# Decoding two layers: all K of batch 6 kept across the layers, one K tile of batch 7 parked in PSUM

## The chip, the cores and the metric

The kernel runs on one core of a Trainium2 chip. The metric is device time in microseconds of one launch. Five engines work beside each other, each with its own queue of instructions: TensorE (PE), VectorE (DVE), ScalarE (ACT), GpSimd (POOL) and SyncE (SP), which here issues all the large DMAs.

## The reference

One decoding step of 8 sequences through an attention block and an MLP block, and then through both again with the same weights and the same caches:

```python
x = x + _A_ref(_layernorm(x, axis=-1), A_k_cache, A_v_cache, A_wq, A_wo)
x = x + _B_ref(_layernorm(x, axis=-1), B_w1, B_b1, B_w2, B_b2)
x = x + _A_ref(_layernorm(x, axis=-1), A_k_cache, A_v_cache, A_wq, A_wo)
x = x + _B_ref(_layernorm(x, axis=-1), B_w1, B_b1, B_w2, B_b2)
```

`_A_ref` is x·wq, attention of 32 query heads over 4 heads of K and V (4096 positions of 128 numbers, float32), then ·wo; `_B_ref` is gelu(x·w1 + b1)·w2 + b2. K and V of one sequence ("batch") are 8 MB each; 8 batches make 128 MB. wq and wo are 16 MB each, w1 and w2 14 MB each. All of it is read once in each layer, but for what stays on the chip from the first layer to the second.

## The kernel before

**The arena.** SBUF holds one area of 52 half tiles. A tile is 128 x 2048 float32, 1 MB: half of the positions of one K or V head of one batch, so a batch has 8 tiles of K and 8 of V; a half tile is 0.5 MB. 48 halves take K, V and weights; the last 4 (`own`) hold rows and probabilities of the softmax, and in between also weights (those whose limit is `ALL`).

**The stream.** `stream` is the list of everything to be loaded, in order. `pump` takes its first piece, finds free halves of the needed number, and issues the DMA on SP; if none are free it stops until `release` frees some. A DMA waits, on SP's queue, for the last reader of its halves, and all later DMAs wait behind it. `CUTS` tells into how many tiles each K or V of a batch is cut: (4, 4) is two DMAs of four tiles.

**The order.** `plan` writes the steps of the attention, one K tile a step; V tiles follow `LAG_V` = 10 steps behind their K. Batches in `AT_ONCE` do all K, the softmax, and then all V. The first layer goes through batches 0 to 7, the second through 7 to 0. So what batches 7 and 6 leave in the arena is used again first: 8 tiles of K 7, 8 of V 7 and 7 of K 6 (`EXTRA`); one of these seven is copied into four PSUM banks (`park_tile`) and back into the arena in the second layer (`unpark`). Besides, the last half tile of wq stays in its own place (`spare`). This leaves 4 halves and the 4 own ones, 4 MB, through which wo, w1, w2 and wq (stages o0, i0, p0, q1) pass in pieces of 1 MB.

**PSUM.** Of eight banks of 512 columns, four hold the parked tile, two are the accumulators of `project`, `expand` and `values` in turn (tag `o`), one holds scores (`s`) and one is for transposes and small sums (`pt`).

**Where the layers meet.** `layernorm` transposes x into bank pt (L168, L169), VectorE copies it out as xnT (L170), one more matmul sums (L174, bank s), and `expand` begins (L235). While q1's second unit runs, `early` scores four K 7 tiles (`first`) and frees them.

Of the kernel before, what the change touches and what calls it, by code (L numbers as in the profile page):

```python
# [33 lines left out]
LAG_V = 10  # L34
# [53 lines left out]
class Kept:  # L88


    def __init__(self, ap):
        self.ap, self.cols = ap, ap.shape[1]

    def free(self):
        pass


@with_exitstack
def decode_layers(ctx: ExitStack, tc: tile.TileContext, x, kc, vc, wq, wo, w1, b1, w2, b2, out):
# [59 lines left out]
    def small_ps(tag):  # L159
        return ps_1.tile([P, CH], F32, tag=tag, name="sps")  # L160
# [4 lines left out]
    def layernorm(xr, rsum):  # L165
        pt = small_ps("pt")
# [9 lines left out]
        nc.vector.tensor_scalar(xc[:, 0:Q4], xr, pm[:, 0:1], None, op0=ALU.add)  # L176
# [35 lines left out]
    def tiles(name):  # L212
        i = 0
        while (name, i) in held:
            yield held.pop((name, i))
            i += 1
        if (*name, "end") in held:
            yield held.pop((*name, "end"))

    def expand(name, unit, rs, finish, hooks={}, last=None):  # L220
        for u in range(2):
            acc = ps_o.tile([P, CH], F32, tag="o", name="acc")
# [4 lines left out]
            for i, slot in enumerate(tiles((name, u))):  # L227
# [13 lines left out]
                if last and u == 1 and at == end:  # L241
                    last(slot.ap)
# [13 lines left out]
    def turned(row, nt):  # L256
        pt = small_ps("pt")
# [28 lines left out]
    def project(name, n_k, lhs, out_row, resid, rsum, hooks={}):  # L286
        y = ps_o.tile([P, CH], F32, tag="o", name="y")
# [15 lines left out]
        nc.vector.scalar_tensor_tensor(out_row, y[:, 0:Q4], 1.0, resid, op0=ALU.mult, op1=ALU.add, accum_out=rsum)  # L303
# [6 lines left out]
    def v_at(b, r):  # L310
        return b, r // NH, r % NH

    def scores(at, kt, spare=False):
        b, j, half = at
        if j == 0:
            st["ps", half] = ps_o.tile([P, CH], F32, tag="o", name="s_ps") if spare else small_ps("s")
# [4 lines left out]
        for g in range(NG):  # L321
            nc.tensor.matmul(ps[32 * g:32 * g + 32, :], qz[:, c:c + 32], kt[:, g * CH:(g + 1) * CH],  # L322
# [11 lines left out]
    def probs(b):  # L334
        pm = small_ps("pt")
# [10 lines left out]
    def turn(b, half):  # L346
# [3 lines left out]
        pp = small_ps("pt")  # L350
# [14 lines left out]
    def values(at, v):  # L365
        b, j, half = at
        if half == 0:
            st["O"] = ps_o.tile([P, CH], F32, tag="o", name="o_ps")
# [13 lines left out]
    def heads(b, j):  # L382
        po = small_ps("pt")
# [14 lines left out]
    def early(key):  # L398
        ap, done = ap_of(key)
        scores(key[1:], ap, spare=key[3] == 1)  # L400
        done()

    def plan(layer, order):

        steps = []
        for i, b in enumerate(order):
            n = i * NR
            whole = b in AT_ONCE[layer]
            steps.append((n + NR - whole, 1, ("probs", b)))
# [7 lines left out]
    def attention(order, keep, done=(), hooks={}):  # L417
        ready = []
        steps = [key for key in plan(st["layer"], order) if key not in done]
        for n, key in enumerate(steps):  # L420
# [27 lines left out]
    def park_tile():  # L448
        spot = ps_k.tile([P, W], F32, name="spot")
# [10 lines left out]
    def unpark(ap):  # L460
        spot = st.pop("spot")
# [131 lines left out]
```

## Time and profile before

| | us |
|---|---|
| median of 3 runs | 875.83 (875.03 to 875.86) |
| the profiled execution, its own time | 875.91 |
| its span from first to last instruction | 874.1 |
| TensorE busy | 540.9 (62%) |
| VectorE busy | 180.7 (21%) |
| ScalarE busy | 48.3 (6%) |
| loads' share of 16 DMA engines' span | 99.2% |

The profile counts an engine as busy only while it works. The DMA row is the mean over 16 DMA engines. The chain of waits goes back from the last instruction, at each step to what released it.

### The profile page before, as it was taken

What the parts mean: (1) busy time and instruction counts of PE and PEld (TensorE: products, weight loads), DVE (VectorE), ACT (ScalarE), POOL (GpSimd) and SP (SyncE); (2) the same over time, 40 slices, a digit from 0 to 9 for tenths busy, and PEclk for the clock granted to TensorE, in tenths of its full rate; (3) what the DMA queues carried; (4) which work ended last, traced back from release to release, by engine and by line L of the source; (5) the groups of instructions that cost most, each with busy time, mean ns of one, the idle gap of its engine ahead of it and who ended that gap; (6) DMA issues with size and microseconds to landing.
All of it is one profiled execution on the core that took longest, in us unless ns stands there. A gap on an engine that the chain in (4) does not pass through costs nothing.

```text
span 874.1 us, 8939 instructions
## 1 busy us (share of the span) xinstructions
PE 540.9 (62%) x3936; PEld 179.6 (21%) x3936; DVE 180.7 (21%) x586; ACT 48.3 (6%) x76; POOL 1.8 (0%) x12
## 2 busy tenths in 40 slices
PE   0557575655766766666757679855676655665655
PEld 0212121211212212222222122211121211222222
DVE  0002222313122322200100124412232313120110
ACT  0100000000000100000000100000000000000000
POOL 0000000000000000000000000000000000000000
PEclk9867778777777876869887889975778777777889
DMA  9999999999999999999999999999999999999997
GB/s 389 439 433 433 432 433 433 432 439 445 432 433 405 422 429 425 413 414 420 422 421 396 423 426 433 427 451 435 436 430 430 432 430 433 429 433 430 431 420 294
DMA packets 19911, 370.61 MB, mean 424 GB/s; under 512 B 2336, under 2 KB 2720, under 8 KB 4128
## 3 DMA queue, kind: packets, MB, share of 16 engines
q1 hardware_dynamic: 19728, 369.91, 99.2%
q8 instruction: 31, 0.51, 0.2%
q10 hardware_dynamic: 144, 0.13, 0.0%
q14 instruction: 8, 0.07, 0.0%
HBM read 369.90 MB, written 0.13 MB: 423 GB/s over the span
## 4 chain that ended last, share of the span: by engine, by line
DMA 76%; PE 18%; DVE 4%; issue 1%; ACT 1%; SPq 0%; ACTq 0%; DVEq 0%
DMA arena<-in_A_v_cache_dram 25%; DMA arena<-in_A_k_cache_dram 24%; DMA arena<-in_B_w_dram 17%; PE sps L322 5%; PE o_ps L372 5%; DMA arena<-in_A_wo_dram 5%; PE acc L235 4%; DMA arena<-in_A_wq_dram 3%; DMA x_row<-in_A_x_dram 3%; PE y L292 2%; DVE scr L377 1%; PE sps L384 1%; PE sps L353 1%; DVE arena L327 1%; DVE scr L375 0%
## 5 line engine op out<-in xcount | busy, mean ns | idle before, releaser
L322 PE MATMUL sps<-arena,qz 128*32 128x512 f32 x992 | 144.2, 708 | 92.4 <-DMA arena<-in_A_k_cache_dram 82.3
L372 PE MATMUL o_ps<-arena 128*32 128x512 f32 x1024 | 158.7, 735 | 26.3 <-DMA arena<-in_A_v_cache_dram 26.3
L292 PE MATMUL y<-arena,oT 128*32 128x256 f32 x960 | 76.6, 463 | 53.2 <-DMA arena<-in_A_wo_dram 30.3
L235 PE MATMUL acc<-arena,xnT 128*32 128x512 f32 (+3 forms) x524 | 82.3, 692 | 43.9 <-DMA arena<-in_B_w_dram 25.3
L377 DVE SCALAR_TENSOR_TENSOR scr<-o_ps,sel_t,scr 128x128 f32<-128x128 f32 x192 | 67.3, 351 | 6.8
L322 PEld LDWEIGHTS sps<-arena,qz 128*32 128x32 f32 x992 | 30.9, 125 | 180.9 <-issue 84.2
L327 DVE TENSOR_SCALAR_CACHE_REDUCE arena<-sps 128x512 f32<-128x512 f32 x31 | 21.4, 691 | 149.3 <-PE sps L322 149.3
L292 PEld LDWEIGHTS y<-arena,oT 128*32 128x32 f32 x960 | 31.5, 127 | 97.2 <-DMA arena<-in_A_wo_dram 34.2
L353 PE MATMUL sps<-ident,arena 128*128 128x128 f32 x128 | 30.7, 385 | 33.1 <-DVE oT L385 16.8
L372 PEld LDWEIGHTS o_ps<-arena 128*32 128x32 f32 x1024 | 31.3, 127 | 96.1 <-issue 67.2
L343 ACT ACTIVATE arena<-arena,bias 128x1024 f32<-128x1024 f32 x16 | 18.4, 1148 | 481.3 <-DVE scr L340 481.3
L384 PE MATMUL sps<-sel_h,scr 128*128 128x8 f32 x128 | 26.2, 277 | 26.8 <-DVE scr L377 23.2
L375 DVE TENSOR_SCALAR scr<-o_ps,sel_t 128x128 f32<-128x128 f32 x64 | 22.4, 351 | 92.2 <-PE o_ps L372 92.2
L235 PEld LDWEIGHTS acc<-arena,xnT 128*32 128x32 f32 x524 | 20.4, 125 | 96.4 <-issue 40.8
L384 PEld LDWEIGHTS sps<-sel_h,scr 128*128 128x128 f32 x128 | 20.3, 200 | 86.4 <-DVE scr L377 66.2
L353 PEld LDWEIGHTS sps<-ident,arena 128*128 128x128 f32 x128 | 19.8, 192 | 42.1 <-ACT arena L343 23.9
L385 DVE TENSOR_TENSOR oT<-sps,scr 128x8 f32<-128x8 f32 x64 | 11.0, 172 | 77.7 <-PE sps L384 77.7
L303 DVE SCALAR_TENSOR_TENSOR x_row<-y,x_row 128x256 f32<-128x256 f32 x4 | 1.7, 425 | 103.0 <-PE y L292 103.0
L359 DVE COPY arena<-sps 128x512 f32<-128x512 f32 x16 | 11.1, 692 | 44.7 <-PE sps L353 44.7
L168 PE MATMUL sps<-ident,x_row 128*128 128x128 f32 x16 | 4.6, 379 | 25.2 <-DMA x_row<-in_A_x_dram 23.5
L336 PE MATMUL sps<-scr,ones 128*128 128x128 f32 x32 | 7.8, 326 | 15.6 <-DVE scr L332 15.6
L361 PE MATMUL sps<-scr,ones 128*128 128x32 f32 x32 | 9.5, 390 | 12.5 <-DVE arena L359 12.5
(72 smaller groups left out, 133.2 us busy)
## 6 DMA issues: line engine op xcount, KB each, us to landing
arena<-in_B_w_dram SPq DMA_DIRECT2D x27, 1024.0 KB, 8.4
arena<-in_A_v_cache_dram SPq DMA_DIRECT2D x10, 2048.0 KB, 28.7
arena<-in_A_wo_dram SPq DMA_DIRECT2D x15, 1024.0 KB, 8.7
arena<-in_A_k_cache_dram SPq DMA_DIRECT2D x7, 2048.0 KB, 30.5
arena<-in_A_wq_dram SPq DMA_DIRECT2D x14, 1024.0 KB, 8.5
arena<-in_B_w_dram SPq DMA_DIRECT2D x2, 7168.0 KB, 44.9
arena<-in_A_k_cache_dram SPq DMA_DIRECT2D x11, 1024.0 KB, 28.1
arena<-in_A_k_cache_dram SPq DMA_DIRECT2D x2, 4096.0 KB, 25.2
```

Of the source, the lines that this page charges most:

```text
L235: nc.tensor.matmul(acc[32 * j:32 * j + 32, d0 - starts[j]:d1 - starts[j]], xnT[:, kt * B:kt * B + 32], slot.ap[:, c + d0 - a:c + d1 - a], ...
L292: nc.tensor.matmul(y[32 * j:32 * j + 32, 0:Q4], lhs[:, kt * B:kt * B + 32], slot.ap[:, c + j * Q4:c + (j + 1) * Q4], start=(kt == 0), stop ...
L322: nc.tensor.matmul(ps[32 * g:32 * g + 32, :], qz[:, c:c + 32], kt[:, g * CH:(g + 1) * CH], start=(j == 0), stop=(j == HKV - 1))
L327: nc.vector.tensor_scalar(st["row", b].ap[:, half * CH:(half + 1) * CH], ps, SCALE, None, op0=ALU.mult, op1=ALU.max, accum_out=st["mx", b] ...
L343: nc.scalar.activation(row, row, AF.Exp, bias=bias, scale=1.0, accum_out=ls)
L353: nc.tensor.transpose(pp[:, t * P:(t + 1) * P], row[:, c:c + P], ident)
L359: nc.vector.tensor_copy(dst, src)
L372: nc.tensor.matmul(o[32 * g:32 * g + 32, :], s[:, g], v[:, g * CH:(g + 1) * CH], start=(half == 0), stop=(half == NH - 1))
L375: nc.vector.tensor_scalar(r, o[:, 0:P], sel_t[:, 0:1], None, op0=ALU.mult)
L377: nc.vector.scalar_tensor_tensor(r, o[:, t * P:(t + 1) * P], sel_t[:, t:t + 1], r, op0=ALU.mult, op1=ALU.add)
L384: nc.tensor.matmul(po[:, 0:REP], r_s[j % 2], sel_h, start=True, stop=True)
L385: nc.vector.tensor_tensor(oT_v[:, j * REP:(j + 1) * REP, b], po[:, 0:REP], rl_s[b % 2][:, j * REP:(j + 1) * REP], ALU.mult)
```

## The change

Three things are moved. All 8 tiles of K 6 stay (one as before in the four PSUM banks). wq's last half tile no longer stays; in its place the first tile of K 7 (`stowed`) is laid down in three parts: its upper half in `spare`, its lower half in the banks s and o1 (`stow`). In the second layer `unstow` brings the two quarters back into a half of the arena, ahead of the last five pieces of wq, and the scores read this tile in four quarters from two places. PSUM tiles are now fixed banks: while o1 is taken, all accumulators are o0, and `layernorm` puts its small sums into bank pt instead of s. And the order: in the first layer V 6 and V 7 follow 16 steps behind their K, so all of K 7 stands ahead of V 6; in the second layer batch 5 goes at once, with V 5 cut into four pieces.

```diff
-LAG_V = 10
-EXTRA = 7
-AT_ONCE = range(6), range(5)
+LAG = {(0, 6): 16, (0, 7): 16}
+AT_ONCE = range(6), range(6)
-    (1, "k", 6): (2, 2, 2, 1, 1), (1, "v", 6): (1, 1, 2, 2, 2), (1, "k", 5): (1, 1, 1, 1, 2, 2), (1, "v", 5): (4, 4), (1, "k", 4): (4, 4),
+    (1, "k", 6): (2, 2, 2, 1, 1), (1, "v", 6): (1, 1, 2, 2, 2), (1, "k", 5): (1, 1, 1, 1, 2, 2), (1, "v", 5): (2, 2, 2, 2), (1, "k", 4): (4, 4),
...
+    spot = psum.tile([P, W], F32, name="spot")
+    bank = {n: psum.tile([P, CH], F32, name=f"bank_{n}") for n in ("o0", "o1", "pt", "s")}
+    turns = {"of": ("o0", "o1"), "n": 0}
+    def next_o():
+        turns["n"] += 1
+        return bank[turns["of"][turns["n"] % len(turns["of"])]]
...
-        pm = small_ps("s")
-        nc.tensor.matmul(pm[:, 0:1], neg_m, rsum, start=True, stop=True)
+        pm = pt[:, Q4:Q4 + 1]
+        nc.tensor.matmul(pm, neg_m, rsum, start=True, stop=True)
...
+        if (st["layer"], key) == (1, stowed):
+            return quarters(held["stowed"].ap) + quarters(spare), lambda: release(held.pop("stowed"))
...
+            lag = LAG[layer, b] if (layer, b) in LAG else 10
...
+    def stow(part):
+        ap, done = ap_of(stowed)
+        if part == 0:
+            nc.scalar.activation(spare, ap[:, SCW:W], AF.Copy)
+        elif part == 1:
+            nc.scalar.activation(bank["s"], ap[:, 0:CH], AF.Copy)
+        else:
+            turns["of"] = ("o0",)
+            nc.scalar.activation(bank["o1"], ap[:, CH:SCW], AF.Copy)
+            done()
+    def unstow(ap):
+        nc.scalar.activation(ap[:, 0:CH], bank["s"], AF.Copy)
+        nc.vector.tensor_copy(ap[:, CH:SCW], bank["o1"])
...
+    stowed = ("k", *k_at(B - 1, 0))
-    kept |= {("k", *k_at(B - 2, r)) for r in range(EXTRA)}
+    kept |= {("k", *k_at(B - 2, r)) for r in range(NR)}
...
-    weights("q1", wq, [[1] * 2 + [2] * 7, [2] * 7 + [1]], [ALL] * 2, (0, SCW))
+    weights("q1", wq, [[1] * 2 + [2] * 7, [2] * 4 + [1] + [2] * 3 + [1]], [ALL] * 2)
+    stream.insert(len(stream) - 5, ("stowed", 1, unstow, ALL, False))
...
-            expand("q0", W, rs, query_unit, last=lambda ap: nc.scalar.activation(spare, ap[:, ap.shape[1] - SCW:], AF.Copy))
-            held["q1", 1, "end"] = Kept(spare)
+            expand("q0", W, rs, query_unit)
+            last = attention(orders[0], kept, hooks={
+                ("k", *k_at(B - 2, NR - 1)): park_tile, stowed: lambda: stow(0),
+                ("turn", B - 1): lambda: (opened(), stow(1)), ("v", *v_at(B - 2, NR - 1)): lambda: stow(2)})
```

The last layer's second `project` also leaves out the row sums that nobody reads.

How the rows move. SP's queue at the end of the first layer's attention, before (128x2048 is one tile, 128x4096 two; the four single K tiles are K 6's last two and K 7's first two):

```order
L205 DMA arena<-in_A_k_cache_dram 128x2048 x4
L205 DMA arena<-in_A_k_cache_dram 128x4096
L205 DMA arena<-in_A_v_cache_dram 128x4096
L205 DMA arena<-in_A_k_cache_dram 128x2048
L205 DMA arena<-in_A_v_cache_dram 128x4096
L205 DMA arena<-in_A_k_cache_dram 128x2048
L205 DMA arena<-in_A_k_cache_dram 128x4096
L205 DMA arena<-in_A_v_cache_dram 128x4096 x5
L205 DMA arena<-in_A_v_cache_dram 128x2048 x2
```

The same place now:

```order
L197 DMA arena<-in_A_k_cache_dram 128x2048 x4
L197 DMA arena<-in_A_k_cache_dram 128x4096
L197 DMA arena<-in_A_k_cache_dram 128x2048 x2
L197 DMA arena<-in_A_k_cache_dram 128x4096
L197 DMA arena<-in_A_v_cache_dram 128x4096 x7
L197 DMA arena<-in_A_v_cache_dram 128x2048 x2
```

The pieces are the same; the last K pieces stand ahead of all V 6. SP's queue from q1 into the second layer's attention, before (128x1024 is a half tile):

```order
L205 DMA arena<-in_A_wq_dram 128x2048 x14
L205 DMA arena<-in_A_wq_dram 128x1024
L205 DMA arena<-in_A_k_cache_dram 128x2048 x4
L205 DMA arena<-in_A_v_cache_dram 128x2048
L205 DMA arena<-in_A_k_cache_dram 128x2048
```

And now:

```order
L197 DMA arena<-in_A_wq_dram 128x2048 x11
L197 DMA arena<-in_A_wq_dram 128x1024
L197 DMA arena<-in_A_wq_dram 128x2048 x3
L197 DMA arena<-in_A_wq_dram 128x1024
L197 DMA arena<-in_A_k_cache_dram 128x2048 x3
L197 DMA arena<-in_A_v_cache_dram 128x2048
L197 DMA arena<-in_A_k_cache_dram 128x2048
```

One half tile of wq comes in, one tile of K 6 goes. TensorE's queue in the layer normalization between p0 and q1, before, with what each row waits for (sps is a bank of tag pt, and for L174 and L183 the bank s):

```order
L168 MATMUL sps<-ident,x_row 128x128 [waits DVE_49]
L169 MATMUL sps<-neg_m,rsum 128x128
L168 MATMUL sps<-ident,x_row 128x128
L169 MATMUL sps<-neg_m,rsum 128x128
L174 MATMUL sps<-rsum,neg_m 128x1 [waits Activation_49]
L235 MATMUL acc<-arena,xnT 32x512 [waits DMAHW4_49,DVE_49]
```

And now:

```order
L160 MATMUL bank_pt<-ident,x_row 128x128 [waits DVE_49]
L161 MATMUL bank_pt<-neg_m,rsum 128x128
L160 MATMUL bank_pt<-ident,x_row 128x128
L161 MATMUL bank_pt<-neg_m,rsum 128x128
L166 MATMUL bank_pt<-rsum,neg_m 128x1 [waits DVE_49]
L225 MATMUL bank_o_67<-arena,xnT 32x512 [waits DMAHW4_49]
```

The wait for VectorE's copy of xnT has moved from the first matmul of `expand` to the small sum ahead of it.

## Rows read from the trace of the kernel before

**Rows 1.** The page: GB/s in 40 slices; the loads' queue: packets, MB, share.
```profile
GB/s 389 439 433 433 432 433 433 432 439 445 432 433 405 422 429 425 413 414 420 422 421 396 423 426 433 427 451 435 436 430 430 432 430 433 429 433 430 431 420 294
...
q1 hardware_dynamic: 19728, 369.91, 99.2%
```

**Rows 2.** The page: shares of the chain that ended last.
```profile
DMA 76%; PE 18%; DVE 4%; issue 1%; ACT 1%; SPq 0%; ACTq 0%; DVEq 0%
```

**Rows 3.** Stretches: length, busy by engine, granted clock, DMA share, GB/s.
```profile
40.00:270.00 230.00, 138.16 (x878) 42.84 (x878) 52.89 (x173) 12.32 (x18) 0.00 (x0) 0.76 1.00 432
395.00:400.00 5.00, 3.48 (x30) 1.65 (x30) 1.35 (x5) 0.66 (x3) 0.00 (x0) 1.00 1.03 420
410.00:460.00 50.00, 31.23 (x279) 10.82 (x278) 4.81 (x16) 1.88 (x3) 0.28 (x1) 0.83 1.01 421
465.00:470.00 5.00, 4.44 (x34) 2.67 (x26) 0.53 (x3) 0.00 (x0) 0.00 (x0) 0.50 1.03 420
470.00:475.00 5.00, 4.85 (x27) 1.14 (x26) 0.64 (x3) 2.05 (x4) 0.00 (x0) 0.84 1.00 395
475.00:480.00 5.00, 2.46 (x16) 0.36 (x16) 0.00 (x0) 0.00 (x0) 0.00 (x0) 0.85 0.98 354
```

**Rows 4.** Timeline of TensorE, end of o0: start, length, line, shapes, idle before.
```profile
391.34 1.93 PE L292 MATMUL y<-arena,oT 128*32 128x256 f32 x16 [0.55 <-DMA arena<-in_A_wo_dram]
393.83 1.07 PE L292 MATMUL y<-arena,oT 128*32 128x256 f32 x16 [0.56 <-DMA arena<-in_A_wo_dram]
395.12 0.64 PE L292 MATMUL y<-arena,oT 128*32 128x256 f32 x8 [0.22 <-DMA arena<-in_A_wo_dram]
396.40 0.64 PE L292 MATMUL y<-arena,oT 128*32 128x256 f32 x8 [0.64 <-DMA arena<-in_A_wo_dram]
```

**Rows 5.** Timeline of TensorE, V 6's last two tiles, then V 5's first four.
```profile
558.24 1.07 PE L372 MATMUL o_ps<-arena 128*32 128x512 f32 x8 [2.24 <-DMA arena<-in_A_v_cache_dram]
...
567.95 1.06 PE L372 MATMUL o_ps<-arena 128*32 128x512 f32 x8 [0.61 <-DMA arena<-in_A_v_cache_dram]
```

**Rows 6.** Timeline of TensorE in p1, the two pieces of 2 MB.
```profile
860.41 1.93 PE L292 MATMUL y<-arena,oT 128*32 128x256 f32 x32 [1.23 <-DMA arena<-in_B_w_dram]
865.32 1.94 PE L292 MATMUL y<-arena,oT 128*32 128x256 f32 x32 [2.98 <-DMA arena<-in_B_w_dram]
```

**Rows 7.** The chain from p0 into q1: start, length, what.
```profile
467.30 0.44 DVE x_row L303 x2
...
470.18 1.76 PE acc L235 x4
473.27 5.28 DMA arena<-in_A_wq_dram
...
493.68 11.48 DMA arena<-in_A_wq_dram
```

**Rows 8.** Timeline of TensorE in that layer normalization.
```profile
469.66 0.43 PE L174 MATMUL sps<-rsum,neg_m 128*128 128x1 f32 x2
```

**Rows 9.** Timeline, the layer normalization between o0 and i0.
```profile
397.11 0.42 DVE L303 SCALAR_TENSOR_TENSOR x_row<-y,x_row 128x256 f32<-128x256 f32 x1 [34.07 <-PE y L292]
...
399.07 1.05 PE L235 MATMUL acc<-arena,xnT 128*32 128x512 f32 x4 [0.20 <-DVE xnT L170]
```

**Rows 10.** Timeline of SP's queue from 467 to 474: first start, length, count.
```profile
467.29 6.31 SPq L205 DMA_DIRECT2D arena<-in_A_wq_dram  x2
```

**Rows 11.** Line 205: time from issue to landing over all its loads.
```profile
DMA to landing us min/median/max: 5.3/12.5/60.4
```

**Rows 12.** The page: DMA issues, count, KB each, median us to landing.
```profile
arena<-in_A_wo_dram SPq DMA_DIRECT2D x15, 1024.0 KB, 8.7
...
arena<-in_A_v_cache_dram SPq DMA_DIRECT2D x2, 4096.0 KB, 30.9
```

**Rows 13.** The page: VectorE's reads of an accumulator; count, busy, mean ns.
```profile
L377 DVE SCALAR_TENSOR_TENSOR scr<-o_ps,sel_t,scr 128x128 f32<-128x128 f32 x192 | 67.3, 351 | 6.8
```

**Rows 14.** Groups by line, VectorE's read of a whole accumulator bank.
```profile
L250 DVE TENSOR_SCALAR scr<-acc,rs 128x512 f32<-128x512 f32 (+1 forms) x8 | 5.5, 682 | 53.7 <-PE acc L235 53.5
```

More of the change, by code (lines that the diff above doesn't have):

```diff
@@ L85, in free @@
             self.arena.freed[self.i + e] = self.arena.clock
[L88 to L95, printed above, removed]
 @with_exitstack
@@ L165, in layernorm @@
     def layernorm(xr, rsum):
-        pt = small_ps("pt")
+        pt = bank["pt"]
         for i in range(2):
@@ L216, in tiles, with expand @@
             i += 1
-        if (*name, "end") in held:
-            yield held.pop((*name, "end"))
-    def expand(name, unit, rs, finish, hooks={}, last=None):
+    def expand(name, unit, rs, finish, hooks={}):
         for u in range(2):
-            acc = ps_o.tile([P, CH], F32, tag="o", name="acc")
+            acc = next_o()
             at = 0
@@ L256, in turned @@
     def turned(row, nt):
-        pt = small_ps("pt")
+        pt = bank["pt"]
         for i in range((nt + 3) // 4):
@@ L315, in scores @@
         if j == 0:
-            st["ps", half] = ps_o.tile([P, CH], F32, tag="o", name="s_ps") if spare else small_ps("s")
+            st["ps", half] = bank["o1" if spare else "s"]
         if j == 0 and half == 0:
@@ L334, in probs @@
     def probs(b):
-        pm = small_ps("pt")
+        pm = bank["pt"]
         nc.tensor.matmul(pm[:, 0:P], ones, dg_s, start=True, stop=True)
@@ L349, in turn @@
             st["S", b] = arena.take(own=True)
-        pp = small_ps("pt")
+        pp = bank["pt"]
         for t in range(T):
@@ L367, in values @@
         if half == 0:
-            st["O"] = ps_o.tile([P, CH], F32, tag="o", name="o_ps")
+            st["O"] = next_o()
         o = st["O"]
@@ L388, in decode_layers, with quarters @@
     pieces = {}
+    def quarters(ap):
+        return [ap[:, g * CH:(g + 1) * CH] for g in range(ap.shape[1] // CH)]
     def ap_of(key):
+        if (st["layer"], key) == (1, stowed):
+            return quarters(held["stowed"].ap) + quarters(spare), lambda: release(held.pop("stowed"))
         name, i = pieces[st["layer"], key] if (st["layer"], key) in pieces else pieces[0, key]
@@ L399, in early @@
         ap, done = ap_of(key)
-        scores(key[1:], ap, spare=key[3] == 1)
+        scores(key[1:], ap if key == stowed else quarters(ap), spare=key[3] == 1)
         done()
@@ L412, in plan @@
                 steps.append((n + r, 0, ("k", *k_at(b, r))))
-                steps.append((n + NR - 1, 3, ("v", *v_at(b, r))) if whole else (n + r + LAG_V, 3, ("v", *v_at(b, r))))
+                steps.append((n + NR - 1, 3, ("v", *v_at(b, r))) if whole else (n + r + lag, 3, ("v", *v_at(b, r))))
         steps.sort(key=lambda e: e[:2])
@@ L432, in attention @@
                 if key[0] == "k":
-                    scores(key[1:], ap)
+                    scores(key[1:], quarters(ap))
                 else:
@@ L533, in decode_layers @@
         expand(f"i{layer}", F // 2, rs, hidden_unit)
-        rsum = row_sums()
+        rsum = None if layer else row_sums()
         project(f"p{layer}", NFT, hT, x_row, x_row, rsum)
```

48 lines of the change are left out of this document (21 added, 27 removed).

## Prediction, before the changed kernel had run

> **What bounds the kernel now.** I read the page's rows on the loads first, then the chain, then the kernel in stretches, and last the timeline where the stretches show less than the usual rate. The loads' queue is busy for 99.2% of 16 engines' span, and brings in 369.91 MB [rows 1]. 76% of the chain that ended last is loads [rows 2]. So the time is the bytes, divided by the rate that their pieces get, plus the few places where the queue runs dry.
>
> The rate depends on how a piece is cut. While K and V come in pieces of 8 MB it is 432 GB/s; in i0 and p0, in pieces of 1 MB, 421 [rows 3]. Where TensorE waits for every piece, its starts give the price: a tile of 1 MB takes 393.83 - 391.34 = 2.49 us, half a tile 396.40 - 395.12 = 1.28 us [rows 4].
>
> One stretch is short of load: 395 and 354 GB/s from 470 to 480, where 421 are usual. That is (26 + 67) x 5 / 421 = 1.1 us of loading lost [rows 3]. Its cause is in the queue: SP issues one load at 467.29 and only one more within 6.31 us, at 473.27 [rows 7, 10]. In between lies the layer normalization between p0 and q1. No half of the arena comes free before q1's first matmuls are done: VectorE has x at 467.30, q1 begins at 470.18, and the load issued at 473.27 lands after 5.28 us, the least of all loads [rows 7, 11]. All other loads have more in front of them. So 5.28 us is what the queue must hold at an issue, about two tiles; the median is 8.7 in o0, and 11.48 at the end of q1 [rows 7, 12]. A delay of TensorE's by less than the difference costs nothing.
>
> **The change part by part.** *Bytes.* K 6's last tile is no longer loaded in the second layer: one tile of 1 MB, -2.49 us. wq's last half tile is loaded a second time: +1.28 us [rows 4]. V 5 comes in four pieces of 2 MB, not two of 4 MB. A piece of 4 MB took 567.95 - 558.24 = 9.71 us [rows 5], one of 2 MB 865.32 - 860.41 = 4.91 [rows 6], so +2 x (2 x 4.91 - 9.71) = +0.2 us. Sum: -1.0 us. These loads stand in an unbroken queue, so the whole of it reaches the end; the bounds are -1.4 (pieces of 2 MB as good as those of 4 MB, half a tile at half the price of a tile) and -0.6 (V 5 twice as dear).
>
> *The layer normalization.* The small sum L174 took 0.43 us on TensorE beside VectorE's copy of xnT (L170) [rows 8]. Both its output and the copy's input are now bank pt, so it waits for the copy, and q1's first matmul stands behind it. That adds 0.43 us and a handover to the chain from 467.30 to 470.18; I take 0.5. Queued behind it on TensorE are all matmuls of q1's first piece, and behind these SP's load of 473.27. There the queue is dry already, so all of it counts: +0.5 us. The same edit stands in the other three normalizations. At the start and in the second layer the loads are of 7 or 8 MB with tens of us in front of them; between o0 and i0 the slack is that of the 8.7 against 5.28 us. There it costs nothing. The bounds: 1.0, if the weights of this sum are loaded in series too; and below nothing, -1.1, all that the stretch loses now. For the chain's length goes with the clock that TensorE is granted: between o0 and i0, at 1.00 of 2.4 GHz, the same steps took 399.07 - 397.11 = 1.96 us, here, at 0.50, the level of 1.2 GHz, 470.18 - 467.30 = 2.88 [rows 3, 7, 9]. I take the nearest row, 0.43, at the clock that this place had.
>
> *One accumulator.* From the first layer's V 7 to the end of q1 every accumulator is bank o0, so a new one waits until VectorE has read the last. For an expansion's second unit that is one read of 0.68 us [rows 14], less what lay there anyway; for each head of V 7, and for o0's first matmul, four reads of 0.351 [rows 13], 1.4 us. A head of V 7 takes two tiles, 5 us of loading, and needs 1.4 us and two tiles of matmuls: TensorE keeps up. All these delays are under the 8.7 - 5.28 = 3.4 us that the queue has in hand: nothing. Without that cover each would cost its own length, 0.7 to 1.4 us at five places.
>
> *Stowing and bringing back.* Three copies on ScalarE in the first layer. ScalarE is idle nearly always there, and only the last of them frees a tile, one that o0's third piece takes. In q1, two copies of 512 columns, on ScalarE and VectorE, each about the 0.68 us of the read above, stand between q1's first piece of unit 1 and the first early scores; VectorE's copy also ahead of the queries' (L267). +0.7 us on TensorE at most. The tile frees half a tile now, not a whole one, and one K tile less stands behind wq: of 11.48 us in front of a load some 2.5 are gone and another 0.7 may be. That leaves 8.3, and 5.28 are needed: nothing.
>
> *K 7 ahead of V 6.* In the first layer the same pieces come in another order, and the slices there show 425 to 431 GB/s and none much below [rows 1]. There is little to gain and, with all of V 6 still to pass through the arena, more than ten us in the queue: nothing. V 5 ahead of K 4's pieces in the second layer: V 5's loads had 30.9 us in front of them [rows 12]: nothing.
>
> Sum: -1.0 + 0.5 = -0.5 us. The profiled execution took 875.91 us, 1.8 us more than its span, and is 0.08 above the median of 875.83. So 875.4 for it, and 875.3 for the median.
>
> Here a rule of the Trainium skill speaks against the change: in "DMA: Bandwidth & Descriptors", section "Anatomy of one DMA", a DMA (measured there for those that GpSimd issues) has a fixed cost of some 2.0 us beside its bytes. The change has two loads more (one tile of K fewer, half a tile of wq and two pieces of V 5 more). The trace of this kernel doesn't bear it out as a cost of each piece: tiles land 2.49 us apart [rows 4], and by the rule, an estimate, 1 MB alone would take 2.0 + 2.4 us. It is a latency here, hidden while another piece is in front.
>
> **The rivals.** *The dry stretch goes.* What decides it is how long TensorE takes from p0's last pieces to q1's first. If that part runs at the higher clock, as between o0 and i0, it is 0.9 us shorter [rows 3, 7, 9], and p0's last matmuls and q1's first with it; the load of 473.27 comes some 2 us earlier, and the 1.1 us aren't lost. For it: the two normalizations are alike in work, and their clocks differ. Against it: the new wait pushes the other way, and what TensorE does ahead of the place is unchanged. Time: -1.0 - 1.1 = -2.1, 873.8 us.
>
> *The queue runs dry in q1, too.* Place: q1's second unit. The tile that comes back takes half a tile of the little room, its scores wait for two copies, and the load behind it needs a whole pair of halves, so it waits for the next piece of wq. Price: nothing until loads there find under 5.28 us in front of them; from then on every us of delay is one of the time. From 8.3 us that needs 3 us of delay; with two such handovers of the room, each up to one piece late (2.49 us), 5 us are possible at most, and 2.5 are a middle. For it: with 4 halves and 4 more it is the narrowest place. Against it: 8.3 us by my count. Time: -0.5 + 2.5 = +2.0, 877.8 us.
>
> *It trades bytes and delays evenly.* The normalization costs 1.0 and V 5's cut 0.6: +-0, 875.8 us. For it: all terms are small, and the bounds meet there.
>
> *Each piece pays its latency.* A mechanism of the rows: a load alone takes 5.28 us, of which 2.49 are its bytes; if the 2.8 us aren't hidden, two more pieces cost 5.6, and the time is 880. Against it: nothing in the rows but the stretch after 470. By the skill's rule named above it would be two times 2.0.
>
> **How the numbers follow.** A measurement of this kernel can't tell less than 0.2%, 1.75 us, from no change. The forecast, 875.3, has 0.57; the dry stretch goes 0.19; even trade 0.15; dry in q1 0.07; latency of each piece 0.02. Of the second, whose 873.8 lies just past the bound of 874.1, some count as no change; in return, the forecast's own lower bound (-1.4 and a part of the 1.1) passes it now and then. Faster 0.18, within 0.2% 0.74, slower 0.08. The likeliest case reaches from 874.3 to 876.4 (-1.4 - 0 and -0.6 + 1.0, each with a little for the runs' own scatter). To leave out no more than 2 in 10, the range takes in the dry stretch's going and a little of the drying in q1: 873.2 to 877.0.
>
> **What would show it.** Right: the loads' queue brings 369.39 MB; K 5's first load lands some 0.7 us earlier than now (-2.49 + 1.28 + 0.5); from L166 to q1's first matmul some 0.4 us more than now; the stretch after 470 at 374 GB/s or less; all else near 421 and 432. Wrong: a second stretch under 400 GB/s, in q1's second unit or in the first layer's V 7; a load there that lands within 5.3 us of its issue; a drying that is gone; or a rate of whole stretches that changed.

## The result and the profile after

| | before | after |
|---|---|---|
| median of the runs side by side | 875.36 us (874.94 to 876.84, 21 runs) | 878.95 us (874.71 to 883.01, 21 runs) |
| ratio after to before, 95% interval | | 1.0039 (1.0026 to 1.0052) |
| profiled execution; its span | 875.91; 874.1 us | 880.35; 878.6 us |
| bytes of the loads' queue; its share | 369.91 MB; 99.2% | 369.38 MB; 98.6% |

The changed kernel is slower by 0.4%, and its runs spread over 8 us where those of before spread over 2. The forecast, 875.3 us and at most 877.0, was wrong. Of all executions in this document one, of 1150.91 us, of a kernel with q1's tiles in halves, was in a slow state and is left out.

The page of after, answering [rows 1]:

```profile
GB/s 387 437 430 430 430 455 436 433 427 427 433 425 421 421 430 426 357 421 419 421 420 416 383 423 428 437 445 428 433 433 427 430 445 425 433 427 433 431 421 264
...
q1 hardware_dynamic: 20016, 369.38, 98.6%
```

The bytes are as forecast. Two slices stand out, 357 and 383, at 1/40 of 878.6 us each: the end of the first layer's attention, and q1. The stretches of after there, with the columns of [rows 3]:

```profile
355.00:360.00 5.00, 3.37 (x17) 0.41 (x16) 1.57 (x5) 0.00 (x0) 0.00 (x0) 0.50 1.02 423
360.00:365.00 5.00, 3.36 (x26) 1.05 (x26) 1.57 (x5) 0.00 (x0) 0.00 (x0) 0.73 0.49 162
365.00:370.00 5.00, 3.79 (x62) 1.73 (x54) 0.17 (x1) 0.00 (x0) 0.00 (x0) 1.00 1.01 398
...
470.00:475.00 5.00, 3.92 (x26) 2.23 (x28) 0.91 (x4) 1.93 (x4) 0.00 (x0) 1.00 1.02 423
475.00:480.00 5.00, 2.72 (x22) 0.32 (x16) 0.16 (x1) 0.13 (x1) 0.00 (x0) 1.00 1.02 411
...
490.00:495.00 5.00, 4.02 (x20) 0.92 (x12) 1.44 (x3) 0.60 (x1) 0.00 (x0) 0.50 1.01 419
495.00:500.00 5.00, 4.54 (x28) 1.37 (x32) 0.47 (x2) 0.00 (x0) 0.00 (x0) 0.58 0.75 308
500.00:505.00 5.00, 5.00 (x48) 1.34 (x39) 1.23 (x1) 2.31 (x2) 0.00 (x0) 1.00 0.97 365
```

Measured against 421 GB/s, 360 to 370 us loses (259 + 23) x 5 / 421 = 3.3 us of loading, and 495 to 505 loses (113 + 56) x 5 / 421 = 2.0. The stretch after 470, which lost 1.1 us before [rows 3], loses only 0.1: here its clock was 1.00, before 0.84 and 0.85, behind a stretch of 0.50.

**The first place** is V 7, the last V of the first layer. TensorE's timeline there (L363 is the values' matmul, L375 a head's sum, L368 VectorE's reads of O, L280 the projection o0):

```profile
342.13 1.93 PE L363 MATMUL bank_o<-arena 128*32 128x512 f32 x8 [2.90 <-DMA arena<-in_A_v_cache_dram]
...
347.73 1.06 PE L363 MATMUL bank_o<-arena 128*32 128x512 f32 x8 [1.64 <-DVE scr L368]
...
352.61 1.94 PE L363 MATMUL bank_o<-arena 128*32 128x512 f32 x8 [1.63 <-DVE scr L368]
354.48 0.60 PE L375 MATMUL bank_pt<-sel_h,scr 128*128 128x8 f32 x2
355.00 1.94 PE L363 MATMUL bank_o<-arena 128*32 128x512 f32 x8
358.57 1.94 PE L363 MATMUL bank_o<-arena 128*32 128x512 f32 x8 [1.63 <-DVE scr L368]
...
364.49 1.93 PE L280 MATMUL bank_o<-arena,oT 128*32 128x256 f32 x32 [1.64 <-DVE scr L368]
```

At a clock of 0.50, the level of 1.2 GHz, a tile takes 1.94 us, and each head after the first waits 1.63 us for VectorE: 358.57 - 352.61 = 5.96 us for the third head, where two tiles load in 2 x 2.49 = 4.98 [rows 4]. From the first head to o0's first matmul it is 364.49 - 342.13 = 22.4 us, and the loads of four heads take 19.9. SP issued o0's first three tiles by 340.14. The fourth needs halves that V 7's last matmul sets free (360.96 + 1.89 = 362.85); it comes at 362.92, first of five within 6.3 us:

```profile
362.92 6.26 SPq L197 DMA_DIRECT2D arena<-in_A_wo_dram  x5
```

By then the queue had nearly run out: 162 GB/s.

**The second place** is q1's second unit. TensorE first, then two of SP's issues:

```profile
491.91 1.94 PE L225 MATMUL bank_o<-arena,xnT 128*32 128x512 f32 x8 [0.87 <-DVE scr L238]
...
495.46 1.06 PE L313 MATMUL bank_s<-arena,qz 128*32 128x512 f32 x2 [0.57 <-DVE qz L255]
...
497.14 1.96 PE L225 MATMUL bank_o<-arena,xnT 128*32 128x512 f32 x8
```

```profile
493.96 0.33 SPq L197 DMA_DIRECT2D arena<-in_A_wq_dram  x1
...
499.15 0.33 SPq L197 DMA_DIRECT2D arena<-in_A_wq_dram  x1
```

The unit waits 0.87 us for VectorE to read the first unit's sums out of the one bank, and everything up to 499 runs at half clock. The first early score is done when the next weights start, at 497.14; it frees half a tile, which no whole tile fits. SP's next issue is at 499.15, right behind the end of the next weights (497.14 + 1.96). 5.2 us without an issue are about as much as the queue held. The shortest time from issue to landing fell from 5.3 us [rows 11] to:

```profile
DMA to landing us min/median/max: 4.7/10.9/60.8
```

In the Trainium skill, "DMA: Bandwidth & Descriptors", section "Anatomy of one DMA", a DMA (measured there for those that GpSimd issues) costs some 2.0 us beside its bytes. 4.7 less the 2.49 of a tile leaves 2.2: the trace agrees for a load with next to nothing in front of it, and not for tiles in a filled queue, 2.49 us apart [rows 4].

**The end.** TensorE fell to half clock in p1's last tiles (a mean of 0.61 from 870 to 876), whose 64 matmuls then outlasted the loads:

```profile
868.64 6.61 PE L280 MATMUL bank_o<-arena,oT 128*32 128x256 f32 x64 [2.96 <-DMA arena<-in_B_w_dram]
...
875.78 0.35 SPq L551 DMA_DIRECT2D out_dram<-x_row  x1
```

The last 2 MB piece's matmuls start 868.64 - 865.32 = 3.3 us later than before [rows 6]. The kernel before lost a little at the two places, too: from 360 to 380 it moved 410 GB/s where the changed one moved 354, and 411 from 500 to 505:

```profile
360.00:380.00 20.00, 12.22 (x130) 4.53 (x130) 0.52 (x2) 0.00 (x0) 0.00 (x0) 0.73 1.01 410
```

So against it the first place costs (67 - 11) x 20 / 421 = 2.7 us and the second 2.0 - 0.1 = 1.9: -1.0 (bytes) - 1.0 (stretch after 470) + 2.7 + 1.9 = +2.6. The other 0.7 of the 3.3 isn't placed. The store is issued 875.78 - 871.42 = 4.4 us later, so the end itself added 1.0; before it was:

```profile
871.42 0.35 SPq L537 DMA_DIRECT2D out_dram<-x_row  x1
```

All together 3.3 + 1.0 = 4.3, against 880.35 - 875.91 = 4.4 measured. The 1.0 at the end goes with the execution and not with the change: behind the last load's landing the store came 2.3 us later here, 1.2 before, but 1.2 in the changed kernel's second profile and 2.3 in the kernel before with the new order (both below).

### The profile page after: what moved, and what is told of

Same layout as the page of the kernel before. It is cut to its first block, busy times and chain, and to the rows that moved or that the text cites. A ratio compares the mean times of both kernels' runs of the same rounds, so it can differ in the third digit from the quotient of the medians.

```text
span 878.6 us, 8957 instructions
## 1 busy us (share of the span) xinstructions
PE 548.7 (62%) x3936; PEld 182.2 (21%) x3936; DVE 181.8 (21%) x586; ACT 50.0 (6%) x79; POOL 1.8 (0%) x12
## 3 DMA queue, kind: packets, MB, share of 16 engines
q1 hardware_dynamic: 20016, 369.38, 98.6%
HBM read 369.38 MB, written 0.13 MB: 421 GB/s over the span
## 5 line engine op out<-in xcount | busy, mean ns | idle before, releaser
L313 PE MATMUL bank_s<-arena,qz 128*32 128x512 f32 x988 | 145.7, 721 | 92.4 <-DMA arena<-in_A_k_cache_dram 81.4
L363 PE MATMUL bank_o<-arena 128*32 128x512 f32 x1024 | 159.6, 741 | 20.8 <-DMA arena<-in_A_v_cache_dram 15.8
L280 PE MATMUL bank_o<-arena,oT 128*32 128x256 f32 x960 | 80.1, 485 | 50.5 <-DMA arena<-in_A_wo_dram 28.1
L225 PE MATMUL bank_o<-arena,xnT 128*32 128x512 f32 (+3 forms) x528 | 81.6, 687 | 41.7 <-DMA arena<-in_B_w_dram 21.9
L313 PEld LDWEIGHTS bank_s<-arena,qz 128*32 128x32 f32 x988 | 32.7, 127 | 188.6 <-issue 91.8
L368 DVE SCALAR_TENSOR_TENSOR scr<-bank_o,sel_t,scr 128x128 f32<-128x128 f32 x192 | 67.3, 350 | 6.8
L280 PEld LDWEIGHTS bank_o<-arena,oT 128*32 128x32 f32 x960 | 32.3, 133 | 97.6 <-DMA arena<-in_A_wo_dram 38.4
L344 PE MATMUL bank_pt<-ident,arena 128*128 128x128 f32 x128 | 30.3, 380 | 33.1 <-DVE oT L376 16.7
L363 PEld LDWEIGHTS bank_o<-arena 128*32 128x32 f32 x1024 | 30.8, 127 | 86.1 <-issue 58.8
L375 PE MATMUL bank_pt<-sel_h,scr 128*128 128x8 f32 x128 | 26.3, 278 | 28.7 <-DVE scr L368 24.8
L375 PEld LDWEIGHTS bank_pt<-sel_h,scr 128*128 128x128 f32 x128 | 20.5, 201 | 87.1 <-DVE scr L368 70.5
```

The source lines that it names most:

```text
L225: nc.tensor.matmul(acc[32 * j:32 * j + 32, d0 - starts[j]:d1 - starts[j]], xnT[:, kt * B:kt * B + 32], slot.ap[:, c + d0 - a:c + d1 - a], ...
L280: nc.tensor.matmul(y[32 * j:32 * j + 32, 0:Q4], lhs[:, kt * B:kt * B + 32], slot.ap[:, c + j * Q4:c + (j + 1) * Q4], start=(kt == 0), stop ...
L344: nc.tensor.transpose(pp[:, t * P:(t + 1) * P], row[:, c:c + P], ident)
L363: nc.tensor.matmul(o[32 * g:32 * g + 32, :], s[:, g], v[:, g * CH:(g + 1) * CH], start=(half == 0), stop=(half == NH - 1))
L368: nc.vector.scalar_tensor_tensor(r, o[:, t * P:(t + 1) * P], sel_t[:, t:t + 1], r, op0=ALU.mult, op1=ALU.add)
L375: nc.tensor.matmul(po[:, 0:REP], r_s[j % 2], sel_h, start=True, stop=True)
```

## The experiments

Medians with the ratio to the kernel before, run on the same chip (95% interval); before's medians there were 875.26 to 875.76.

| kernel | median us (range) | ratio |
|---|---|---|
| changed, two accumulators in V 7 | 876.53 (875.12 to 879.96) | 1.0018 (1.0008 to 1.0029) |
| changed, way back earlier on ScalarE | 877.69 (874.81 to 882.4) | 1.0029 (1.0014 to 1.0044) |
| changed, old order of loads | 887.39 (884.59 to 888.83) | 1.0125 (1.0111 to 1.0140) |
| before, new order of loads | 875.17 (875.01 to 876.06) | 0.9997 (0.9989 to 1.0006) |
| changed, both of the first two | 877.78 (876.19 to 880.13) | 1.0023 (1.0014 to 1.0032) |
| both, copy one head earlier | 876.6 (874.64 to 878.93) | 1.0011 (1.0001 to 1.0021) |
| the same kernel again | 877.47 (874.31 to 880.32) | 1.0021 (1.0008 to 1.0034) |
| the same, tiles of q1 in halves | 876.35 (874.06 to 879.80) | 1.0006 (0.9991 to 1.0020) |
| the same, two accumulators in q1 | 875.91 (874.64 to 878.15) | 1.0005 (0.9996 to 1.0014) |
| the same, both of these | 875.49 (874.12 to 879.53) | 0.9998 (0.9989 to 1.0006) |
| before, small sum in bank pt | 875.46 (875.07 to 876.46) | 1.0000 (0.9991 to 1.0009) |
| before, one accumulator in q1 | 875.34 (875.05 to 878.05) | 1.0002 (0.9994 to 1.0011) |

One kernel measured twice differs by 0.1%, so steps of that size between the changed variants tell nothing by themselves. A profile is of one execution; its clocks need not be those of the median.

### Two accumulators in V 7

```diff
-                ("turn", B - 1): lambda: (opened(), stow(1)), ("v", *v_at(B - 2, NR - 1)): lambda: stow(2)})
+                ("turn", B - 1): lambda: (opened(), stow(1)), ("v", *v_at(B - 1, NR - 1)): lambda: stow(2)})
```

> The changed kernel, with one edit: the tile's last quarter goes into bank o1 after the last V 7 tile, not after the last V 6 tile, so that V 7 has two accumulators again. Theory (one accumulator): in the profile of the changed kernel a head of V 7 took 5.96 us at the lower clock, more than the 4.9 us in which its two tiles land, so TensorE ended V 7 6 us after its last tile, no half came free, and loading fell to 162 GB/s from 360 to 365 (2.4 to 3.2 us). With two accumulators the dip at o0's start goes: 2 to 3 us faster than the changed kernel, about 876 to 877, the dip in q1 stays. Rival (order): TensorE is slow in V 7 because its work now comes in small portions at the lower clock; then V 7 stays late and the time stays at 879.

Measured 876.53. TensorE's timeline in V 7 shows the heads waiting for loads again, not for VectorE; only o0's first matmul still does:

```profile
346.70 1.06 PE L363 MATMUL bank_o<-arena 128*32 128x512 f32 x8 [0.94 <-DMA arena<-in_A_v_cache_dram]
...
351.61 1.28 PE L363 MATMUL bank_o<-arena 128*32 128x512 f32 x8 [2.52 <-DMA arena<-in_A_v_cache_dram]
...
359.93 1.07 PE L280 MATMUL bank_o<-arena,oT 128*32 128x256 f32 x16 [1.63 <-DVE scr L368]
```

The heads are 4.9 us apart, the pace of the loads, and 2.4 us of the median came back; the ratios' difference, 0.0021, is just clear of its own uncertainty, by the two intervals some 0.0017. From 355 to 360, where the copy into o1 now stands, 336 GB/s still lose 1.0 us.

But this profile had the full clock for much of V 7 (0.95 from 345 to 350, 0.93 from 355 to 360), so it alone can't tell accumulator from clock. Two profiles of kernels that have an edit in q1 besides, long after V 7, can. With two accumulators at half clock (both edits, below) the heads keep the pace of the loads, 351.44 - 346.53 = 4.9 us, and wait for them:

```profile
346.53 1.94 PE L363 MATMUL bank_o<-arena 128*32 128x512 f32 x8 [1.43 <-DMA arena<-in_A_v_cache_dram]
...
351.44 1.76 PE L363 MATMUL bank_o<-arena 128*32 128x512 f32 x8 [0.59 <-DMA arena<-in_A_v_cache_dram]
```

With one accumulator and mostly the full clock (the next kernel, in an execution of 874.89 us) two heads still wait for loads; the last, at full clock, takes 361.30 - 357.29 = 4.0 us, less than its tiles' 4.98:

```profile
346.82 1.06 PE L363 MATMUL bank_o<-arena 128*32 128x512 f32 x8 [2.03 <-DMA arena<-in_A_v_cache_dram]
...
351.74 1.93 PE L363 MATMUL bank_o<-arena 128*32 128x512 f32 x8 [1.74 <-DMA arena<-in_A_v_cache_dram]
...
357.29 1.07 PE L363 MATMUL bank_o<-arena 128*32 128x512 f32 x8 [1.64 <-DVE scr L368]
...
361.30 1.93 PE L280 MATMUL bank_o<-arena,oT 128*32 128x256 f32 x32 [1.63 <-DVE scr L368]
```

There 360 to 370 loses (57 + 8) x 5 / 421 = 0.8 us, not 3.3. So the first place takes both: one accumulator, and half clock.

### The way back earlier, on ScalarE alone

```diff
-        nc.vector.tensor_copy(ap[:, CH:SCW], bank["o1"])
+        nc.scalar.activation(ap[:, CH:SCW], bank["o1"], AF.Copy)
...
-    weights("q1", wq, [[1] * 2 + [2] * 7, [2] * 4 + [1] + [2] * 3 + [1]], [ALL] * 2)
-    stream.insert(len(stream) - 5, ("stowed", 1, unstow, ALL, False))
+    weights("q1", wq, [[1] * 2 + [2] * 7, [2] * 3 + [1] + [2] * 4 + [1]], [ALL] * 2)
+    stream.insert(len(stream) - 6, ("stowed", 1, unstow, ALL, False))
```

> The changed kernel, with one edit in q1: the parked tile is brought back one piece of wq earlier, and both quarters by ScalarE, so that VectorE's queue holds no copy ahead of the queries. Theory (the way back stands on the path): in the changed kernel's profile 5.2 us pass between the loads issued at 493.96 and at 499.15, in which TensorE waits for the quarters, the queries and the early scores; with the copies done earlier the dip to 308 and 365 GB/s around 500 goes: 1.5 to 2 us faster, about 877, and the dip at o0's start stays. Rival (room): one K tile and half a tile fewer are in the queue's hands there; then the dip stays, and the time with it, 879.

Measured 877.69; its interval overlaps much of the changed kernel's, so a gain is not shown. Its profile, of one of its two fastest executions, had the clock at 1.00 from 490 to 505 and lost 0.3 us from 495 to 505; at that clock it can't tell what the edit is worth.

### The order of the loads, undone and alone

```diff
-LAG = {(0, 6): 16, (0, 7): 16}
+LAG = {}
```

> The changed kernel with the first layer's order undone (V 6 and V 7 again 10 steps behind their K; the second layer as changed). Theory (one accumulator): V 7 still has one bank, so TensorE still ends V 7 late: dip at o0's start as now or a little larger, since V 7 now begins late as well; 879 to 881. Rival (order): the dip goes, 876 to 877.

> The kernel before with the new order in the first layer alone (all of K 7 ahead of V 6), two accumulators kept. Theory (one accumulator): the order costs nothing, 875.4 within 0.3. Rival (order): loading dips at o0's start here as well, 877 to 878.

Undone in the changed kernel, 887.39; alone in the kernel before (its lag for batches 6 and 7 of the first layer set to 16), 875.17. The order costs nothing by itself. With the old order the same wait is dearer, and dearer than the 879 to 881 expected; one stretch of that kernel:

```profile
365.00:370.00 5.00, 3.36 (x26) 0.66 (x18) 1.57 (x5) 0.00 (x0) 0.00 (x0) 0.84 0.00 0
```

No byte moved for 5 us. Its heads come at the same 361.59 - 355.63 = 5.96 us, with the same wait of 1.63. Why the queue ran so much emptier wasn't followed further.

### Both edits, and the copy one head earlier

The first has both edits above. The second also moves the hook of `stow(2)` to `v_at(B - 1, NR - 3)`, behind the last reader of o1.

> Both earlier edits together: the stowing copy into o1 only after V 7 (two accumulators during V 7), and the way back from PSUM on ScalarE alone, one tile earlier, with the half-size tile of q1 put in one place sooner. Theory that the two dips add (each edit gave back its own: 878.95 to 876.53 is 2.4 us, 878.95 to 877.69 is 1.3 us): 878.95 - 2.4 - 1.3 = 875.3 us. Rival, that both edits gave back the same microseconds because a late stream is late only once: no better than the first alone, 876.5 us. Second rival, that with both dips gone the saved 1.0 us of bytes shows: 874.3 us.

> As the run with both edits, but the copy into o1 (and with it the free half tile) comes after the last head of V 7 but one, which is the last reader of o1, one head (about 4.9 us) sooner than after the last. V 7 keeps two accumulators. Theory that the dip of about 1 us left at the first o0 loads of the first experiment is SP waiting for that half tile: it goes, 0.5 to 1 us below the run with both edits, 874.3 to 874.8 us. Rival, that the dip is the S tile or the matmul of y that waits 1.63 us for VectorE: same as the run with both edits.

> The kernel with the copy one head earlier once more, beside the last one on the same chip, for its spread and a second profile. Its first profile had tiles 2.44 to 2.49 us apart through o0, layernorm and q1 and lost nothing there (last landing 869.49, of before 870.21). Theory: median 876 to 877 us again; if this profile is of a run near 877 us or above, its missing time is one or two gaps of 1 us between landings within 465 to 530 us, where the clock is near 0.5. Rival, that the gaps lie elsewhere (before 465 or after 530 us).

877.78, and 876.6 and 877.47 for the second kernel's two measurements: the theory that the gains add (875.3) fell, and so did 874.3 to 874.8 for the second. What remained is seen in the second kernel's two profiles, of spans 873.5 and 878.5 us. First the shorter, then the longer, same columns as above:

```profile
470.00:475.00 5.00, 3.87 (x24) 1.28 (x28) 0.52 (x2) 2.05 (x4) 0.00 (x0) 1.00 1.01 408
475.00:480.00 5.00, 2.21 (x24) 0.32 (x16) 0.00 (x0) 0.00 (x0) 0.00 (x0) 1.00 1.00 410
...
495.00:500.00 5.00, 4.10 (x36) 0.79 (x24) 1.22 (x1) 2.31 (x2) 0.00 (x0) 1.00 0.99 410
500.00:505.00 5.00, 2.13 (x16) 0.32 (x16) 0.00 (x0) 0.00 (x0) 0.00 (x0) 0.99 1.00 415
```

```profile
470.00:475.00 5.00, 4.68 (x17) 1.59 (x20) 0.75 (x3) 2.06 (x4) 0.00 (x0) 0.50 0.95 392
475.00:480.00 5.00, 2.93 (x24) 0.77 (x16) 0.00 (x0) 0.00 (x0) 0.00 (x0) 0.96 0.80 292
...
495.00:500.00 5.00, 5.00 (x28) 1.34 (x32) 0.00 (x0) 0.00 (x0) 0.00 (x0) 0.58 0.73 269
500.00:505.00 5.00, 4.97 (x44) 1.49 (x36) 1.22 (x1) 2.31 (x2) 0.00 (x0) 1.00 0.95 326
```

One kernel, two clocks: with 0.50 from 470 to 475 and 0.58 from 495 to 500 the longer run loses (29 + 129 + 152 + 95) x 5 / 421 = 4.8 us in these four stretches, the shorter, at 1.00, (13 + 11 + 11 + 6) x 5 / 421 = 0.5. That is 4.3 of the 5 us between them. In the longer, TensorE was busy for all of 495 to 500.

### The changed kernel once more

> The changed kernel unaltered, for a second profile. Theory that the loss sits at two places whose size the granted clock sets: V 7's heads again start 5.9 us apart where the clock is near 0.5 and the rate falls below 200 GB/s at 360:365; the second dip at 495:505 and the one before q1 may be larger or smaller by 1 to 2 us than in the first profile. Rival, that the loss is spread over the stream: the same rates at these places, and lower ones elsewhere.

Unaltered, 879.0 us and a span of 877.2. From 360 to 380 it moved 354 GB/s and from 480 to 500 391, as in the first profile (354 and 392): the losses sit at the two places.

### The small sum alone

```diff
-        pm = small_ps("s")
-        nc.tensor.matmul(pm[:, 0:1], neg_m, rsum, start=True, stop=True)
+        pm = pt[:, Q4:Q4 + 1]
+        nc.tensor.matmul(pm, neg_m, rsum, start=True, stop=True)
...
```

The normalization's second small sum stays in bank s.

> The kernel before with one line of the change alone: the small sum of layernorm in bank pt, behind the copy that reads pt, instead of in bank s. Theory of the prediction: the small sum waits for the copy and for nothing that q1's first loads need, up to +0.5 us where TensorE is at half clock, so 875.4 to 875.9 us. Rival: no cost at all, 875.3 us, since the copy is done before the weights' matmuls anyway.

No cost that can be told: 875.46. The half us forecast lies within the interval, so this run doesn't refute it either.

### One accumulator in q1: undone, and alone

Undone, in the kernel with the copy one head earlier:

```diff
-            st["ps", half] = bank["o1" if spare else "s"]
+            st["ps", half] = bank["o0" if spare else "s"]
...
         nc.scalar.activation(ap[:, CH:SCW], bank["o1"], AF.Copy)
+        turns["of"] = ("o1",)
```

Alone, in the kernel before:

```diff
-            acc = ps_o.tile([P, CH], F32, tag="o", name="acc")
+            if (name, u) != ("q1", 1):
+                acc = ps_o.tile([P, CH], F32, tag="o", name="acc")
```

> The kernel with the copy one head earlier, and q1's second unit accumulates in o1 as soon as the stowed quarter has been copied out of it (its early scores of the second half go to o0), so that it need not wait for VectorE to read the first unit's sums out of o0. In the last profile that wait was 0.93 us with TensorE at half clock, and 5 us of full TensorE time behind it let the queue run dry at 498 us. Theory that one accumulator in q1 is what is left over: median 874.6 to 875.4 us, with the spread of before (2 us). Rival, that only the clock decides (half speed between 490 and 500 us makes 5 us of work that loads can't wait for, with either accumulator): 876.5 to 877.5 us and a spread of 4 to 6 us.

> The kernel before with one thing of the change: q1's second unit accumulates in the bank of the first and waits until VectorE has read it. Theory that this wait is what spreads the changed kernel's runs: median 876 to 877 us, with runs above 878. Rival, that the spread comes from the fuller arena (the loads of q1 issued later because two slots are held), with this wait hidden: 875.4 us and the spread of before.

Undone: 875.91, level with before, but its interval also overlaps that of the same kernel with one accumulator (877.47). And the edit trades the wait for another: the unit's first matmul now waits for ScalarE's copy out of o1, 1.17 us where it was 0.93 for VectorE:

```profile
490.66 1.07 PE L225 MATMUL bank_o<-arena,xnT 128*32 128x512 f32 x8 [1.17 <-ACT arena L469]
```

This profile had the clock at 1.00 from 490 to 505, so it doesn't test the wait at half clock. Alone: 875.34; the wait by itself shows no cost. Whether it hurts together with the rest of the change isn't shown. The profile of the kernel before with one accumulator shows what is different there; TensorE and SP, then its stretch:

```profile
489.46 1.93 PE L236 MATMUL acc<-arena,xnT 128*32 128x512 f32 x8 [0.87 <-DVE scr L251]
...
493.00 1.93 PE L323 MATMUL sps<-arena,qz 128*32 128x512 f32 x8 [0.57 <-DVE qz L268]
```

```profile
491.45 0.33 SPq L205 DMA_DIRECT2D arena<-in_A_wq_dram  x1
...
494.99 0.33 SPq L205 DMA_DIRECT2D arena<-in_A_wq_dram  x1
```

```profile
495.00:500.00 5.00, 5.00 (x42) 1.41 (x37) 0.46 (x1) 1.50 (x2) 0.00 (x0) 0.83 1.00 392
500.00:505.00 5.00, 2.97 (x32) 0.81 (x28) 0.76 (x1) 0.81 (x1) 0.00 (x0) 1.00 1.00 396
```

The same wait of 0.87 us and half clock as in the changed kernel (0.50 up to 495, then 0.83 where that had 0.58), but the first early score frees a whole tile, and SP issues right behind it (493.00 + 1.93, 494.99): 3.5 us after its last issue, not 5.2. It loses (29 + 25) x 5 / 421 = 0.6 us where the changed kernel loses 2.0.

### The tiles of q1 in halves, and all edits together

```diff
-    weights("q1", wq, [[1] * 2 + [2] * 7, [2] * 3 + [1] + [2] * 4 + [1]], [ALL] * 2)
-    stream.insert(len(stream) - 6, ("stowed", 1, unstow, ALL, False))
+    weights("q1", wq, [[1] * 2 + [2] * 7, [2] * 3 + [1] * 10], [ALL] * 2)
+    stream.insert(len(stream) - 10, ("stowed", 1, unstow, ALL, False))
```

The last kernel has this and the two accumulators in q1.

> As the run with the copy one head earlier, but the tiles of q1's second unit behind the place of the stowed tile come in halves of 0.5 MB (ten instead of one half, four whole and one half), so that every freed half can be loaded at once. Price by the rows of o0's tiles (two halves 2.51 to 2.56 us against 2.49 for a whole): about 4 times 0.05, 0.2 us. Theory that what is left (876.6 against the 874.6 of its best run) is lost in q1's second unit to halves that wait for a neighbour: median 875.0 to 875.6 us and a smaller spread. Rival, that it is lost at layernorm before q1 and at the half clock wherever it falls: 876.6 us or, with the smaller tiles, 876.8 us.

> All edits together: two accumulators in V 7 with the copy into o1 after the last head but one, the way back on ScalarE before q1's second unit, that unit accumulating in o1, and its later tiles in halves. Theory of two causes in q1 (the accumulator and the freed half that no whole tile fits): 874.8 to 875.3 us, its best runs at 874.0 to 874.3 (the 1.0 us of bytes saved, less 0.2 us for the halves). Rival, one cause, the accumulator alone: 875.9 to 876.1 us as in the run with o1 in q1. Rival, the clock at layernorm before q1 (1.1 to 1.2 us where it is near 0.5, in before too): a spread of 2 us and more that neither edit narrows, median near 875.5.

876.35, beside 877.47 for the same kernel with whole tiles on the same chip (the intervals overlap), and 875.49 with all edits: 0.9998 of before, no faster. Its best run is 874.12, 0.9 below the best of before beside it (874.98), which fits the saved bytes; best runs alone don't prove it. The profiled execution of this last kernel was its slowest, 879.53; its stretches:

```profile
475.00:480.00 5.00, 3.23 (x24) 0.68 (x16) 0.00 (x0) 0.00 (x0) 0.00 (x0) 0.94 0.83 277
...
495.00:500.00 5.00, 4.53 (x25) 1.11 (x28) 0.47 (x2) 0.00 (x0) 0.00 (x0) 0.55 1.00 356
500.00:505.00 5.00, 4.65 (x44) 1.24 (x36) 1.23 (x1) 2.31 (x2) 0.00 (x0) 1.00 0.91 281
```

At half clock the place after 470 and q1's second unit run dry even so, the second by (65 + 140) x 5 / 421 = 2.4 us. The halves are not shown to help.

Put side by side, the profiles of the changed variants say what the loss in q1's second unit goes with. Where the clock from 490 to 500 was 0.50 to 0.58, 495 to 505 loses 2.0 us (the changed kernel, twice), 2.9 (copy one head earlier, the longer run) and 2.4 (all edits). Where it was 1.00, it loses 0.3 at most: two accumulators in V 7, way back earlier, both, copy one head earlier (the shorter run), and two accumulators in q1. In between, at 0.66 and then 1.00, the halves alone lose 0.9. At full clock SP's pause at this place is 493.72 - 490.64 = 3.1 us, not 5.2, with one accumulator and whole tiles (the shorter run).

## Why the prediction was wrong

- **One accumulator: the step that failed.** It said that a head of V 7 takes 5 us of loading and needs 1.4 us and two tiles of matmuls, so "TensorE keeps up". The two tiles were never priced. A tile at the two clocks took 1.93 and 1.07 us already in o0 [rows 4]. At the lower one a head takes 355.00 - 352.61 = 2.39 us for its first tile and the head sum, 1.94 for its second and 1.63 of waiting for VectorE's reads: 5.96, not under 4.98. At the higher one it would have kept up, 4.0. A pace slower than the loads isn't one delay under the 3.4 us in hand; it adds up head by head until the queue is dry. Two accumulators in V 7 gave 2.4 us of the 3.6 back. In the Trainium skill, "Perfetto Trace Analysis", section "Matmuls", independent groups should rotate through banks, so that reading one out lies beside the next one's matmuls. The trace agrees in V 7 (5.96 against 4.9 us a head, both at half clock); in q1 of the kernel before a single bank showed no cost (875.34).
- **Stowing and bringing back: also too cheap.** The rival "the queue runs dry in q1, too" named place and price (2.5 us; 2.0 measured) and got 0.07. I took the queue's lead from the end of q1, 11.48 us, where the tile comes back earlier, and treated the freed half as room. There SP found nothing to issue for 5.2 us. At full clock that pause is 3.1 and the rival's loss doesn't come.
- **The layer normalization: chain right, loss larger at half clock.** At the same clock of 0.50 the way from the first matmul of the normalization to q1's is 470.94 - 468.03 = 2.91 us in the longer profile of the kernel with the copy one head earlier:

```profile
468.03 0.79 PE L160 MATMUL bank_pt<-ident,x_row 128*128 128x128 f32 x2 [0.55 <-DVE x_row L294]
...
470.94 1.92 PE L225 MATMUL bank_o<-arena,xnT 128*32 128x512 f32 x4
```

  Before, it was 470.18 [rows 7] - 467.79 = 2.39, so +0.5, as forecast:

```profile
467.79 0.80 PE L168 MATMUL sps<-ident,x_row 128*128 128x128 f32 x2 [0.56 <-DVE x_row L303]
```

  The loading lost is more than that. With the clock at 0.50 from 465 to 475 the changed variants (both edits, copy one head earlier in the longer run, and the last two with both accumulators in q1) lost 1.8 to 2.1 us from 470 to 480. The kernel before, at 0.50 up to 470 and then 0.84, lost 1.1: +0.7 to 1.0, up to the stated bound of 1.0. What parts the narrower room and the longer stay at half clock have in it isn't separated. In the profile of after the place had the full clock and the dry stretch went, the rival's case; but this is the execution and not the change: the kernels before with the small sum in pt, with the new order and with one accumulator in q1 moved about 419 GB/s there at 1.00 from 470 to 475. Their spans, single executions of 873.7, 874.3 and 873.8 against 874.1, don't show the 1.1 us at the end.
- **Bytes and order: right.** 369.38 MB against 369.39; 0.9997 for the order alone. The slices at the end of the first layer's attention were misread, 405 to 429 and not 425 to 431 GB/s [rows 1]; nothing hung on it.
- **Chances.** All delays were judged one by one against one spare time. Two of them exceeded it, at half clock, and that clock had been read for the normalization alone. Two of the stated signs of being wrong came: stretches under 400 GB/s in V 7 and in q1's second unit, and a load within 5.3 us of its issue (4.7). The last rival's own sum was off: 875.3 + 5.6 is 880.9, not 880.

What stays open: why TensorE gets half clock in V 7, after 465 and from 490 to 500 us in some executions and not in others, and how the loss in q1 at half clock divides between the accumulator and the room in the arena.

## What to carry to other kernels

Price a loop's pace on the engine that waits at the lower clock that its stretch can get, reads of the accumulator included, and compare it with the pace of the loads: a shortfall per step adds up, and a fixed slack in a queue doesn't cover it for long. Read the queue's lead at the place that is changed, and count freed room only in the sizes that the next load can use. A second PSUM bank for an accumulator can be worth more than the tile that it could store.

## What the runs showed of the hardware

One kernel's executions, with the same instructions, lay 5 us apart (spans 873.5 and 878.5), with the granted clock as the visible difference: 1.00 against 0.50 from 470 to 475 and from 490 to 495, 1.00 against 0.58 from 495 to 500. The kernel before had 0.50 from 465 to 470 as well [rows 3] and its runs spread over 2 us. A load with next to nothing in front of it took 4.7 us for 1 MB; in a filled queue such loads landed 2.49 us apart.
